# Every second first-layer product tile of a fused attention and FFN kernel moves to another PSUM bank, from unit 34 on

## The chip, the core and the metric

One core of one Trainium2 chip runs the whole program. The metric is the device time of one execution in microseconds. The engines are named as in the profile: PE multiplies matrices, PEld is its weight load, DVE is the vector engine, ACT the scalar engine, POOL the general-purpose engine and SP the engine that issues most transfers.

## What is computed

```python
scores = (1.0 / np.sqrt(D)) * np.matmul(q, k.transpose(0, 1, 3, 2))     # B, H, S, D = 4, 8, 576, 64
x = (np.log1p(abs(pos_i - pos_j)) / np.log1p(max(pos_i, 1)))[..., None]
bias = np.maximum(x @ w1 + b1, 0.0) @ w2                                # 576 x 576, 8 heads, 32 hidden
scores = scores + bias.transpose(2, 0, 1)[None]
attn = softmax(scores)
x = np.matmul(attn, v)                    # heads joined: 4 x 576 rows of 512
xn = (x - mu) / np.sqrt(var + 1e-06) * g_ln
out = x + np.maximum(xn @ w_ch1, 0.0) @ w_ch2                           # 512 -> 2048 -> 512
```

## The kernel before, in words

The 576 query rows of a batch are cut into four chunks of 128 and a tail of 64. A *unit* is one batch, one chunk and one head (for a tail, two heads); there are 144. For each unit `qk` makes the score products (L391, tile `sps`, two buffers of two banks), DVE adds the bias and takes the minimum (L434), ACT takes the exponential (L438) and a half-precision copy (L443), DVE makes the remainder of that copy (L462, L464), a transfer transposes both (L470) and `pv` multiplies by the values (L480, tile `xps`, one bank). `pv` of a unit stands three, from unit 38 four units behind. When the eight heads of a chunk are through, the 128 rows are scaled (L516, for tails L543) and normalised and become one of 18 *blocks*.

The FFN works on a block in four jobs. A job is a first-layer tile and a second-layer step. `ffn_w1` accumulates 48 products of 128 columns into one 128 x 512 PSUM tile `hps` (L709), ACT writes its ReLU in half precision to `hh` (L714), and DVE writes the remainder of that rounding (L717, the closure `lo`, called a step later). Only then is the bank of `hps` free. `ffn_w2` multiplies `hh` by the second-layer weights in 12 products of 512 columns into the tile `y` (L736, tag `y0`), and DVE adds `y` to the residual (L747). `ffn_micro` alternates the two: with two tiles open the older one's `ffn_w2` comes before the next `ffn_w1`. There are 72 `hps` tiles in all.

The bias is made in 36 groups of 16 rows. `bias_relu` fills four `r` tiles on DVE and ACT; in the next step `bias_mm` multiplies them (L181: eight product instructions, 32 output partitions each), and two ACT instructions move the result to `ev` (L187), which goes to memory (`nb`) and is read back per unit as `ldb`. The tiles `r`, `ev` and the softmax tile `t` share one pool of seven buffers. From the 13th group on a group of at most 512 columns is held in the PSUM tag `y1`; the last such group comes near unit 100.

PSUM is full: four banks for `sps`, one for `xps`, one with the tag `h`, one with `y0`, one with `y1`. Before the change the tag `h` holds every `hps` tile (and a few small ones), and `y1` holds sums over the weights at the start and then these bias products only.

The program is written unit by unit. A planner of the tile framework then lays out each engine's order when the kernel is built: an instruction whose buffer or input is not there by the planner's own clock is passed by later ones of the same engine. On the chip that order is fixed, and each engine takes its instructions in it.

Of the kernel before, what the change touches and what calls it, by code (L numbers as in the profile page):

```python
# [8 lines left out]
F32 = mybir.dt.float32  # L9
# [13 lines left out]
def kernel(  # L23
# [35 lines left out]
    ps_h = ctx.enter_context(tc.tile_pool(name="ps_h", bufs=1, space=bass.MemoryType.PSUM))  # L59
    ps_y = ctx.enter_context(tc.tile_pool(name="ps_y", bufs=1, space=bass.MemoryType.PSUM))  # L60
# [545 lines left out]
    ustep = [-1]  # L606
# [89 lines left out]
        V.tensor_scalar(out=gs_sb, in0=gs_sb, scalar1=gsc, scalar2=4.0, op0=ALU.mult, op1=ALU.mult)  # L696
        V.tensor_scalar(out=ginv, in0=ginv, scalar1=0.25, scalar2=None, op0=ALU.mult)

    yps = {}

    def ffn_w1(k, fs):
        n = 128 * len(blocks[k])
        h = ps_h.tile([128, 512], F32, tag="h", name="hps")
        for idx, f in enumerate(fs):
            w = wslot[f].bitcast(F16)
            i = 0
            for kk in range(4):
                for wo, xo in ((0, 0), (0, 4), (512, 0)):
                    T.matmul(out=h[:, idx * n:idx * n + n],  # L709
                             lhsT=w[:, wo + kk * 128:wo + kk * 128 + 128],  # L710
                             rhs=xT[k][:, xo + kk, 0:n], start=(i == 0), stop=(i == 11))
                    i += 1
        hh = hp.tile([128, 2, 512], F16, tag="h", name="hh")
        S.activation(hh[:, 0], h, AF.Relu)  # L714

        def lo():
            V.scalar_tensor_tensor(out=hh[:, 1], in0=h, scalar=0.0, in1=hh[:, 0],  # L717
                                   op0=ALU.max, op1=ALU.subtract)

        return [k, fs, hh, lo]  # L720
# [62 lines left out]
    def ffn_micro(u):  # L783
        if state["w1"] and len(pend) > 1:
            k, fs, hh, _ = pend.pop(0)
            ffn_w2(k, fs, hh)
            state["w1"] = False
            return True
        kf = next_fs(u)
        if kf:  # L790
            flush_lo()
            pend.append(ffn_w1(*kf))
            state["lo"] = pend[-1][3]
            state["w1"] = True
            return True
        if pend:
            flush_lo()
            k, fs, hh, _ = pend.pop(0)
            ffn_w2(k, fs, hh)
            state["w1"] = False  # L800
            return True
        return False
# [189 lines left out]
```

## Time and profile before

| what | value |
|---|---|
| three runs | 683.54, 686.28, 686.31 us (median 686.28) |
| profiled execution | 679.99 us, of which the span from first to last instruction is 678.2 us |
| mean granted TensorE clock | 0.985 of 2.4 GHz |
| PE busy | 647.7 us (96% of the span) |
| DVE, ACT, POOL busy | 457.8, 392.0, 97.4 us |

Busy times are sums over the whole span. A share of the span is an average over stretches with different limits, so the stretches are looked at one by one. Unit 34 begins at about 192 us, where its L434 starts.

### The profile page before, as it was taken

How to read it: one execution, taken by the hardware profiler on the slowest of the kernel's cores; microseconds unless marked ns; L12 is line 12 of the kernel's file. 1: busy time of each engine (PE TensorE's matmuls, PEld its weight loads, DVE VectorE, ACT ScalarE, POOL GpSimd, SP SyncE). 2: the span in 40 equal slices, each digit the busy share in tenths (PEclk: the TensorE clock that was granted, in tenths of full speed). 3: DMA queues.
4: the chain of work that ended last, by engine and by line, in shares of the span. 5: the costliest groups of instructions: out<-in, count | busy, mean ns of one | idle time of the engine just before them, and what ended most of it. 6: DMA issues, size and time to landing. Idle time of an engine off the chain costs nothing.

```text
span 678.2 us, 19142 instructions
## 1 busy us (share of the span) xinstructions
PE 647.7 (96%) x7929; PEld 448.4 (66%) x7929; DVE 457.8 (68%) x1061; ACT 392.0 (58%) x777; POOL 97.4 (14%) x163
## 2 busy tenths in 40 slices
PE   6889996998999889999899999999999999999997
PEld 4447774676466666666667766666776677677775
DVE  6588999778757567686766575757576676766322
ACT  5565847478957447787764577576554455444110
POOL 5312321011000011111101110111011120000000
PEclk9989997899999999999899999999999999999999
DMA  8999885444659996868869789789996976744100
GB/s 312 294 404 331 307 294 161 143 91 115 143 122 148 223 246 156 173 156 164 172 149 239 134 183 181 136 197 181 201 200 144 166 153 125 121 98 87 33 16 17
DMA packets 186955, 117.24 MB, mean 173 GB/s; under 512 B 163956, under 2 KB 164084, under 8 KB 186868
## 3 DMA queue, kind: packets, MB, share of 16 engines
q1 hardware_dynamic: 177124, 81.00, 55.8%
q0 software_dynamic: 9600, 34.84, 16.6%
q8 instruction: 62, 1.02, 0.6%
q10 hardware_dynamic: 144, 0.18, 0.1%
q14 instruction: 25, 0.20, 0.1%
HBM read 60.51 MB, written 15.63 MB: 112 GB/s over the span
## 4 chain that ended last, share of the span: by engine, by line
PE 50%; DVE 0%; ACT 0%; issue 0%
PE hps L709 19%; PE y L736 18%; PE sps L391 6%; PE xps L480 6%; PE bps L181 1%; DVE v L369 0%; DVE x L747 0%; DVE e L462 0%; ACT e L443 0%; DVE x L516 0%; ACT t L438 0%; DVE e L464 0%
## 5 line engine op out<-in xcount | busy, mean ns | idle before, releaser
L709 PE MATMUL hps<-xT,w 128*128 128x128 f16 x3240 | 196.4, 220 | 5.8 <-DVE hh L717 2.6
L709 PEld LDWEIGHTS <-w 128*128 128x128 f16 x3240 | 184.6, 98 | 11.5 <-issue 5.2
L736 PE MATMUL y<-w,hh 128*128 128x512 f16 x810 | 189.1, 381 | 1.9 <-ACT hh L714 1.8
L438 ACT ACTIVATE t<-t,m 128x576 f32<-128x576 f32 x144 | 111.0, 771 | 132.8 <-DVE m L434 132.2
L736 PEld LDWEIGHTS <-hh 128*128 128x128 f16 x864 | 79.7, 98 | 90.6 <-ACT hh L714 3.3
L462 DVE SCALAR_TENSOR_TENSOR e<-t,e 128x512 f16<-128x512 f32 x120 | 82.8, 690 | 81.8 <-ACT e L443 81.5
L434 DVE CUSTOM_DVE_ANT_0 t<-sps,ldb 128x576 f32<-128x576 f32 x144 | 105.9, 753 | 31.4 <-PE sps L391 21.2
L391 PE MATMUL sps<-kf,qf 64*128 64x288 f32 (+1 forms) x640 | 96.6, 436 | 3.5 <-DVE m L434 3.5
L443 ACT ACTIVATE e<-t 128x576 f16<-128x576 f32 x120 | 80.8, 679 | 9.8 <-DMA pt<-e 3.5
L714 ACT ACTIVATE hh<-hps 128x512 f16<-128x512 f32 x72 | 42.0, 583 | 53.4 <-PE hps L709 47.9
L717 DVE SCALAR_TENSOR_TENSOR hh<-hps,hh 128x512 f16<-128x512 f32 x72 | 49.4, 687 | 34.0 <-ACT hh L714 33.5
L391 PEld LDWEIGHTS sps<-kf,qf 64*128 64x128 f32 (+1 forms) x640 | 48.2, 176 | 35.6 <-issue 17.5
L480 PEld LDWEIGHTS <-pt 128*128 128x128 f16 (+1 forms) x1456 | 49.3, 100 | 30.5 <-issue 24.9
L747 DVE SCALAR_TENSOR_TENSOR x<-y,ycs,x 128x512 f32<-128x512 f32 x58 | 43.4, 748 | 32.2 <-PE y L736 32.0
L480 PE MATMUL xps<-v,pt 128*128 128x64 f16 (+1 forms) x1456 | 59.0, 195 | 1.9 <-DMA pt<-e 1.1
L291 POOL DMA_DIRECT2D kf<-in_k_s_dram x56 | 31.1, 556 | 161.4 <-PE sps L391 114.3
L304 POOL DMA_DIRECT2D qf<-in_q_main_dram x32 | 18.5, 577 | 162.4 <-PE xps L480 82.6
L187 ACT ACTIVATE ev<-bps,cb_sb,par_sb 128x144 f32<-128x144 f32 (+27 forms) x48 | 26.0, 593 | 26.2 <-PE bps L181 26.0
L160 ACT ACTIVATE r<-psi_sb,par_sb 128x448 f32<-128x448 f32 (+23 forms) x72 | 39.7, 614 | 0.0
L569 POOL TENSOR_SCALAR rs<-mv 128x1 f32<-128x1 f32 x18 | 9.9, 549 | 146.3 <-DVE mv L568 138.3
L438 ACT ACTIVATION_READ_ACCUMULATOR t<-t,m 128x1 f32 x144 | 27.0, 188 | 0.0
L181 PE MATMUL bps<-r,nw_sb 128*32 128x448 f32 (+24 forms) x200 | 26.9, 494 | 0.0
(121 smaller groups left out, 641.4 us busy)
## 6 DMA issues: line engine op xcount, KB each, us to landing
kf<-in_k_s_dram POOLq DMA_DIRECT2D x56, 288.0 KB, 4.8
w<-in_w_ch_dram SPq DMA_DIRECT2D x22, 512.0 KB, 8.7
ldb<-nb SPq DMA_DIRECT2D x32, 288.0 KB, 4.5
qf<-in_q_main_dram POOLq DMA_DIRECT2D x32, 256.0 KB, 4.6
nb<-ev SPq DMA_DIRECT2D x24, 296.0 KB, 3.4
vf<-in_v_p_dram POOLq DMA_DIRECT2D x16, 320.0 KB, 7.5
out_dram<-x SPq DMA_DIRECT2D x18, 256.0 KB, 2.1
wend<-in_w_ch_dram SPq DMA_DIRECT2D x8, 512.0 KB, 4.8
```

The costliest lines, as they stand in the source:

```text
L160: S.activation(r[:, 0:n], psi_sb[:, 0:n], AF.Relu, bias=pr_sb[:, g4:g4 + 1], scale=1.0)
L391: m = T.matmul(out=o, lhsT=l, rhs=kk, start=True, stop=True, tile_position=(64 * hf, 64 * e))
L434: ttri[u] = V.tensor_tensor_reduce(out=halves(t), in0=ps[:, :, 0:HS], in1=halves(bias), scale=-0.125, scalar=3e38, op0=ALU.add, op1=ALU.mi ...
L438: S.activation(t, t, AF.Exp, bias=m, scale=-1.0, accum_out=l8[b, c][:, h:h + 1])
L443: S.activation(e16[:, 0:SEQ], t, AF.Copy, scale=E_SCALE)
L462: V.scalar_tensor_tensor(out=e16[:, 640:1152], in0=t[:, 0:512], scalar=E_SCALE, in1=e16[:, 0:512], op0=ALU.mult, op1=ALU.subtract)
L480: T.matmul(out=o, lhsT=p[:, m], rhs=v[:, j, a, :], start=(i == 0), stop=(i == len(ops) - 1))
L709: T.matmul(out=h[:, idx * n:idx * n + n], lhsT=w[:, wo + kk * 128:wo + kk * 128 + 128], rhs=xT[k][:, xo + kk, 0:n], start=(i == 0), stop=( ...
L714: S.activation(hh[:, 0], h, AF.Relu)
L717: V.scalar_tensor_tensor(out=hh[:, 1], in0=h, scalar=0.0, in1=hh[:, 0], op0=ALU.max, op1=ALU.subtract)
L736: T.matmul(out=yps[k][t], lhsT=hh[:, a, o:o + 128], rhs=w[:, wo:wo + 512], start=(f == f0 and i == 0), stop=(f == f1 - 1 and i == 2))
L747: V.scalar_tensor_tensor(out=x, in0=y, scalar=ycs[:, g:g + 1], in1=x, op0=ALU.mult, op1=ALU.add)
```

## The change

The tiles of `ffn_w1` are counted. While the unit counter is at 34 or more, each one with an even number takes the PSUM bank of the tag `y1` in place of `h`. No instruction is added or taken away.

```diff
-    yps = {}
+    yps, hn = {}, [0]
 
     def ffn_w1(k, fs):
         n = 128 * len(blocks[k])
-        h = ps_h.tile([128, 512], F32, tag="h", name="hps")
+        hn[0] += 1
+        if ustep[0] >= 34 and hn[0] % 2 == 0:
+            h = ps_y.tile([128, 512], F32, tag="y1", name="hps")
+        else:
+            h = ps_h.tile([128, 512], F32, tag="h", name="hps")
         for idx, f in enumerate(fs):
```

## Rows read from the trace of the kernel before

**Rows 1.** Busy time by stretch: length, engines, clock, DMA share, GB/s.
```profile
192.00:336.00 144.00, 138.47 (x1861) 93.59 (x1859) 98.41 (x234) 99.40 (x202) 18.00 (x31) 0.99 0.84 173
336.00:480.00 144.00, 144.00 (x1839) 99.93 (x1837) 94.23 (x220) 91.34 (x180) 18.81 (x32) 0.99 0.84 174
480.00:678.20 198.20, 194.39 (x2458) 139.06 (x2455) 110.69 (x245) 76.10 (x149) 17.77 (x27) 1.00 0.57 113
...
330.00:340.00 10.00, 8.00 (x113) 6.30 (x110) 8.77 (x19) 7.21 (x13) 2.11 (x3) 0.83 0.83 148
```

**Rows 2.** PE's waits from 192 us on: us in total, times, longest.
```profile
PE hps L709 <- DVE hh L717: 2.6, 2, 1.3
PE y L736 <- ACT hh L714: 1.6, 1, 1.6
```

**Rows 3.** Chain that ended last, two units near 512 us: start, us, what.
```profile
511.87 1.17 PE sps L391 x8
513.04 0.52 PE xps L480 x14
513.56 2.68 PE hps L709 x48
516.24 0.41 PE xps L480 x14
516.64 2.59 PE y L736 x12
```

**Rows 4.** Timeline near 517 us, how the tile of rows 3 is emptied.
```profile
516.37 0.58 ACT L714 ACTIVATE hh<-hps 128x512 f16<-128x512 f32 x1
517.24 0.68 DVE L717 SCALAR_TENSOR_TENSOR hh<-hps,hh 128x512 f16<-128x512 f32 x1
```

**Rows 5.** Timeline 223 to 237 us, the first wait for the bank.
```profile
223.80 0.58 ACT L714 ACTIVATE hh<-hps 128x512 f16<-128x512 f32 x1
224.67 0.69 DVE L717 SCALAR_TENSOR_TENSOR hh<-hps,hh 128x512 f16<-128x512 f32 x1
225.41 2.84 PE L709 MATMUL hps<-xT,w 128*128 128x128 f16 x48 [1.28 <-DVE hh L717]
...
230.21 2.01 SPq L470 DMA_TRANSPOSE wend<-e  x1
...
236.10 0.63 PE L480 MATMUL xps<-v,wend 128*64 128x64 f16 x28 [0.53 <-DMA wend<-e]
```

**Rows 6.** Timeline 250 to 254 us, the second wait for the bank.
```profile
250.19 2.17 PE L709 MATMUL hps<-xT,w 128*128 128x128 f16 x36 [1.30 <-DVE hh L717]
250.72 0.75 DVE L434 CUSTOM_DVE_ANT_0 t<-sps,ldb 128x576 f32<-128x576 f32 x1
251.39 0.75 DVE L434 CUSTOM_DVE_ANT_0 t<-sps,ldb 128x576 f32<-128x576 f32 x1
252.46 0.86 DVE L543 TENSOR_TENSOR x<-xps,rl 64x256 f32<-64x256 f32 x2
253.47 0.63 PE L480 MATMUL xps<-v,pt 128*64 128x64 f16 x28 [0.43 <-DVE x L543]
```

**Rows 7.** All first-layer remainders from 192 us on: busy, mean ns, idle before.
```profile
L717 DVE SCALAR_TENSOR_TENSOR hh<-hps,hh 128x512 f16<-128x512 f32 x64 | 44.0, 687 | 32.8 <-ACT hh L714 32.3
```

**Rows 8.** PE's groups from 336 to 472 us, the bias products.
```profile
L181 PE MATMUL bps<-r,nw_sb 128*32 128x385 f32 (+7 forms) x64 | 7.6, 545 | 0.0
```

**Rows 9.** Timeline, bias products behind a first-layer tile, first and last of six.
```profile
203.60 0.80 PE L181 MATMUL bps<-r,nw_sb 128*32 128x352 f32 x8
205.56 0.69 DVE L717 SCALAR_TENSOR_TENSOR hh<-hps,hh 128x512 f16<-128x512 f32 x1
...
462.20 1.04 PE L181 MATMUL bps<-r,nw_sb 128*32 128x497 f32 x8
462.94 0.69 DVE L717 SCALAR_TENSOR_TENSOR hh<-hps,hh 128x512 f16<-128x512 f32 x1 [0.96 <-ACT hh L714]
463.18 0.58 PE L480 MATMUL xps<-v,pt 128*128 128x64 f16 x14
```

**Rows 10.** Timeline near 349 us, a bias group ahead of a tile.
```profile
349.58 1.09 ACT L187 ACTIVATE ev<-bps,cb_sb,par_sb 128x384 f32<-128x384 f32 x2 [2.67 <-PE bps L181]
350.75 1.45 PE L709 MATMUL hps<-xT,w 128*128 128x128 f16 x23
```

**Rows 11.** Bias additions on DVE from 192 us on, and what they waited for.
```profile
L434 DVE CUSTOM_DVE_ANT_0 t<-sps,ldb 128x576 f32<-128x576 f32 x110 | 80.4, 753 | 25.4 <-PE sps L391 21.2 <-DMA nb<-ev 3.9
```

## The prediction

> **What bounds the kernel now.** I read the busy times by stretch first, from 192 us, where the change can first act. PE is the engine to watch: it is busy for 138.47 of the 144 us up to 336 us, for all of the next 144, and for 194.39 of the last 198.2, and the missing 3.8 there are the last residual addition and the transfer of the result behind PE's last product [rows 1]. So from 192 us on PE is idle for 144 − 138.47 = 5.5 us that a change could give back, all of it before 336 us.
>
> A busy PE could still hide slack, so I looked at one period of the chain that ended last. Two units, one first-layer tile and one second-layer step take 1.17 + 0.52 + 2.68 + 0.41 + 2.59 = 7.37 us, with no hole between them; the first layer runs at 2.68 / 48 = 55.8 ns a product, the second at 2.59 / 12 = 216 ns [rows 3]. 128 columns at 2.4 GHz would be 53 ns and 512 would be 213 ns, so the products themselves leave about 5% and 1%.
>
> PE's waits come third. The wait that the second bank addresses is a first-layer product waiting for the DVE remainder of the tile before, which empties bank `h`: 2.6 us in two waits of 1.3. The one larger single wait, 1.6 us, is a second-layer product waiting for ACT's ReLU, and no bank frees that [rows 2].
>
> Why are there only two? In the period above the tile's last product ends at 516.24, its ReLU runs 516.37 to 516.95 and its remainder ends at 517.92 [rows 3, 4]. The next tile starts one period after this one, at 513.56 + 7.37 = 520.93. The bank has been free for 3.0 us by then: `pv`, the second layer and the next scores lie between.
>
> **The change, part by part.** *Removed:* no instruction; the wait for `h`. First wait: ACT's ReLU came late, at 223.80, the remainder at 224.67, and PE stood 1.28 us to 225.41 [rows 5]. With two banks the tile in question finds its bank long empty. But what is late next? PE's following wait is for the transpose into `wend`, issued at 230.21, which releases `pv` at 236.10 after 0.53 us of idle PE [rows 5]. If PE comes there 1.28 us earlier and the transpose does not, it stands 1.81 us and nothing is won. Second wait: 1.30 us, to 250.19. Between it and the next wait DVE works back to back (L434 at 250.72 and 251.39, then L543 at 252.46), and `pv` is released by that L543 at 253.47 after 0.43 us of idle PE [rows 6]. DVE would not be earlier, so PE would stand 1.73 us there. The saving is thus between 0 and 2.6 us. I take 0, the value that both next waits point to.
>
> *Added, bias products behind a tile:* bank `y1` now has two users. A bias group that follows an even-numbered tile must wait for that tile's remainder. I laid the old order over the new banks: six groups start on PE while an even tile is still in the bank. The first starts at 203.60, against a remainder that ends at 205.56 + 0.69 = 206.25: 2.65 us. The last starts at 462.20 against 462.94 + 0.69 = 463.63: 1.43 us [rows 9]. The four between give 1.43, 1.44, 1.43 and 1.01 in the same way, so 9.4 us if every group stood in its old place. Behind it in PE's queue would stand `pv` (0.58 us), then the second layer and the scores, which need none of this bank [rows 3, 9]. The first three of the six lie before 331 us, ahead of the 1.6 us wait on ACT, and can partly run out in it [rows 2]. The last three, after 336 us, have no idle time to run out in: 1.43 + 1.01 + 1.43 = 3.9 us.
>
> Lower bound: the planner knows the bank is taken and puts `pv` and the second layer ahead. 0.58 + 2.59 = 3.17 us of such work is more than the longest of these waits, 2.65, so the cost can be 0. Then the bias comes up to some 3 us later; it is read back many units later, and the four `r` buffers are held longer in a pool of seven. If that cover is gone, L434 waits for a buffer: it already did for 3.9 us in the whole stretch, and PE had no wait for it [rows 2, 11].
>
> *Added, tiles behind a bias group:* a tile in `y1` must wait for both L187 of the group before. Near 349 us these end at 349.58 + 1.09 = 350.67, and the tile began at 350.75, 0.08 us later [rows 10]. It fits in the old order, but barely.
>
> *Value taken:* between 0 and 9.4 us I go by how the planner's order has held for the same kind of hand-over. After 192 us the bank `h` passes from one tile to the next 63 times (64 tiles [rows 7]), and PE waited 2.6 us for it in all [rows 2]: 0.041 us a hand-over. In `y1` there are eight bias groups from 336 to 472 us (64 instructions, eight a group [rows 8]) and nine even tiles between them, so 17 hand-overs where PE has no other idle time: 17 × 0.041 = 0.7 us.
>
> *Moved:* no transfer and no DVE or ACT instruction is added, and none gets longer. After the last bias group, near unit 100, the second bank is used freely, in a stretch where PE waits for nothing.
>
> Sum on the profiled execution: 679.99 − 0 + 0.7 = 680.7 us. That execution lies 6.3 us below the median of the runs shown, so I add the change to the median: 686.28 + 0.7 = 687.0 us. A difference of 0.5%, 3.4 us, is about the least that can be told here: the runs shown lie 2.8 us apart, and the profiled one further off.
>
> **Rule and row.** The trace shows a bank hand-over with 3.0 us to spare in the steady period [rows 3, 4]. The Trainium skill, "TensorE: Matmul & The Clock Gate", section "HAM oscillation — how this bites in real kernels", reports that double-buffering PSUM gave a kernel that was already kept busy no further gain (126.6 against 125.5 us, 0.9%). The rows agree so far; by that rule alone the sum would stay where it is.
>
> The same skill, "Perfetto Trace Analysis", section "Matmuls" under "Optimizing Tensor Performance", says the opposite for a case like this: rotate independent product groups through different banks, so that emptying one overlaps the next. By that rule the forecast would be the first rival's. The trace bears it out at two places in 486 us.
>
> **The rivals.**
> 1. *Faster: the second bank loosens the planner's order.* First-layer tiles no longer wait for the bank on the planner's clock either, so they can fill every hole that PE has before 336 us. All 5.5 us go, and with them the drop of the clock that the holes near 331 us bring: between 330 and 340 us the granted clock is 0.83 [rows 1], so 10 × (1 − 0.83) = 1.7 us are lost. Gain 5.5 + 1.7 = 7.2 us: 679.1. For it: the order is laid anew from unit 34, and runs slower than the profiled one may have more such holes. Against it: at 331 us `ffn_w2` follows its own tile with no other tile open, so there is nothing to fill in, and after 336 us there is no hole at all. It counts as faster from 3.4 us, about half of it.
> 2. *Slower: bias products stand at the head of PE's queue.* The place is the six groups above; the price is 9.4 us if the planner's clock frees the bank earlier than the chip does, as it did for the tile of the wait at 224 us, whose remainder came late: 695.7. With the last three alone it is 3.9 us: 690.2. It decides from 3.4 us, a little over a third of 9.4. Against it: later products are free to go ahead.
> 3. *No effect at all:* the planner's order stays as it is and each hand-over fits: 686.3, which is the same verdict as the forecast.
>
> **How the numbers follow.** The forecast with rival 3 gets 0.53: PE is full after 336 us, and both waits that go are followed by waits that PE does not set. Faster gets 0.25: a new order may close more holes than the two. Slower gets 0.22: hand-overs that fit by 0.08 us can slip. The predicted time is 687.0. The range runs from rival 1's 679 to 692, a little over rival 2's smaller case, and leaves out its full 9.4 us; within the forecast's own case it is 683.5 to 690.
>
> **What would show it.** In the trace after, the waits of first-layer products for L717 near 224 and 250 us should be gone and the next waits of `pv` longer by about as much. Bias products should stand behind `pv` or second-layer products where they followed a tile. New waits of L181 for L717, or of L709 for L187, should sum to under 2 us after 336 us. PE should be as busy after 336 us, with the same end. The prediction is wrong if PE's idle time between 192 and 336 us falls well below 5.5 us with the span shorter by as much (rival 1), or if L181 stands on PE for more than 3 us in all (rival 2). A new order on DVE or ACT, with PE waiting for scores or transposes, would be a cause that I have not priced.

## The result, and the profile after

The changed kernel takes 692.17 us in the median of six runs (689.74 to 695.26), against 684.60 us for six runs of the kernel before (681.02 to 686.31): a ratio of 1.0133 with a 95% interval from 1.0089 to 1.0178. It is slower by 1.3%, about 9 us. The forecast was 687.0 us and no difference; the median lies just above its range. In the file after, the lines from `ffn_w1` on are four higher: products L713, ReLU L718, remainder L721, second layer L740, residual L751.

The profiled execution took 695.26 us with a span of 693.5 us, 15.3 us more than the profiled span before. Where do they arise? The additions of the bias on DVE mark the units. First the kernel before, from unit 34 on: count, shortest, median and longest in ns, then the first and the last start in us.

```profile
L434 DVE CUSTOM_DVE_ANT_0 t<-sps,ldb x110: 747/753/759, 192.2 to 616.9; 128x576 f32<-128x576 f32 x110
```

The same view of the kernel after:

```profile
L434 DVE CUSTOM_DVE_ANT_0 t<-sps,ldb x110: 743/752/759, 194.3 to 632.2; 128x576 f32<-128x576 f32 x110
```

Unit 34 starts 194.3 − 192.2 = 2.1 us later, before the change can act: that much belongs to these two executions, not to the change. The 110 additions take 437.9 us in place of 424.7, so 13.2 us arise behind it. Behind the last addition both need 61.3 us (678.2 − 616.9 and 693.5 − 632.2). By the starts of single units the stretch from unit 104 to unit 140, behind the last bias group, is also the same, 132.9 us before and 132.8 after. So the second bank used freely costs nothing and gains nothing there, where PE waited for nothing before either. The whole loss lies ahead of unit 104: 2.9 us in units 34 to 47, 6.5 in 48 to 72 and 4.5 in 80 to 103, while units 73 to 79, which have no bias group, took 0.7 us less. These are single executions. From unit 34 to unit 104 the kernel before took 283.3 us, and two experiments below in which PE has nearly the same order, e1 and e13, took 279.9 and 279.7; the kernel after took 296.5.

The busy time by stretch of the kernel after answers to [rows 1]; columns as there:

```profile
194.00:336.00 142.00, 133.78 (x1790) 90.38 (x1788) 90.51 (x217) 92.06 (x192) 16.45 (x30) 0.99 0.82 167
336.00:480.00 144.00, 138.64 (x1720) 94.09 (x1721) 90.43 (x210) 84.87 (x167) 17.71 (x31) 0.99 0.82 166
...
357.00:361.00 4.00, 3.44 (x14) 1.51 (x15) 2.22 (x7) 3.97 (x9) 0.00 (x0) 0.62 0.37 82
```

PE stood for 8.2 us up to 336 us and for 5.4 us in the next 144, where before it had stood for none: 13.6 against 5.5, so 8.1 of the 13.2 us are idle time. The other 5.1 us are time in which PE is busy for longer: 654.2 us in all, 6.5 more than before, 1.3 of it ahead of unit 34. The third line shows one source: for four microseconds behind a long wait the granted clock was 0.62 of 2.4 GHz, so for most of them it was at the lower level, 1.2 GHz. The kernel after has a second such stretch (0.66 from 258 to 263 us), but the kernel before had one too (0.83 from 330 to 340 us [rows 1], where the kernel after has 1.00), so the clock makes a difference of one stretch, about 1.7 us. The larger source is the bias products. This is their line in the kernel before (busy, mean ns of one, idle before):

```profile
L181 PE MATMUL bps<-r,nw_sb 128*32 128x448 f32 (+24 forms) x200 | 26.9, 494 | 0.0
```

and in the kernel after:

```profile
L181 PE MATMUL bps<-r,nw_sb 128*32 128x448 f32 (+24 forms) x200 | 29.9, 495 | 6.7 <-DVE hh L721 3.4 <-ACT r L160 3.2
```

One product takes as long as before, but together they keep PE busy for 3.0 us more, since at a few places the eight products of a group are pulled apart and overlap less. I did not account for what is left.

PE's waits from 194 to 480 us in the kernel after (us in total, times, longest) answer to [rows 2]:

```profile
PE bps L181 <- DVE hh L721: 3.4, 2, 2.0
PE bps L181 <- ACT r L160: 3.2, 1, 3.2
PE xps L480 <- DVE x L543: 2.3, 1, 2.3
PE xps L480 <- DMA wend<-e: 2.0, 1, 2.0
PE hps L713 <- DMA xT<-x: 1.0, 1, 1.0
PE y L740 <- DVE x L751: 0.7, 1, 0.7
```

The waits of a first-layer product for the remainder, 2.6 us, are gone. In their place bias products wait 6.6 us, half for a tile's remainder and half for their own input `r`, and `pv` waits 4.3 us for a transpose and for DVE.

The timeline of the kernel after shows three of these places:

```profile
323.86 0.83 PE L713 MATMUL hps<-xT,wend 128*128 128x128 f16 x12
...
329.19 0.57 ACT L718 ACTIVATE hh<-hps 128x512 f16<-128x512 f32 x1
...
330.80 0.80 PE L181 MATMUL bps<-r,nw_sb 128*32 128x353 f32 x8 [1.37 <-DVE hh L721]
...
356.89 0.62 ACT L160 ACTIVATE r<-psi_sb,par_sb 128x385 f32<-128x385 f32 x1 [4.91 <-DMA nb<-ev]
357.56 1.10 PE L181 MATMUL bps<-r,nw_sb 128*32 128x385 f32 x2 [3.19 <-ACT r L160]
...
465.12 1.01 PE L181 MATMUL bps<-r,nw_sb 128*32 128x481 f32 x8 [2.02 <-DVE hh L721]
```

The first is what the forecast priced for a bias group behind an even tile, 1.0 to 2.65 us at each of six groups [rows 9]. The bias does not stand right behind the tile: the planner had put a second-layer step, scores and part of `pv` between. But the tile's last product ended at 324.69, and its ReLU, behind other work in ACT's order, came only at 329.19, so the remainder ended 6.05 us after the product. The second is not a wait for the bank at all. ACT stood 4.91 us, because `r` needs one of the pool's seven buffers and the next one to come free held an `ev` that was still being written to memory. The third looks like the first, but the chain that ended last leads further back (start, us, what):

```profile
454.99 1.19 ACT r L160 x2
...
456.20 4.30 DMA nb<-ev
...
460.63 0.13 DVE t L434
...
464.46 0.61 DVE hh L721
...
465.12 1.01 PE bps L181 x8
```

L434 on DVE needed a buffer of the same pool, which the write held to 460.5 us; the exponential and the copy on ACT and the halves of that copy on DVE followed, the remainder that empties the bank came behind them, and behind the remainder stood the bias products on PE. Before the change this chain had no place on the path: ACT's `r` waited for no buffer, and the 3.9 us of L434 [rows 11] did not reach PE.

### The profile page after: what moved, and what is told of

Read it like the earlier page. It is cut to its first block, busy times and chain, and to the rows that moved or that the text cites. A ratio compares the mean times of both kernels' runs of the same rounds, so it can differ in the third digit from the quotient of the medians.

```text
span 693.5 us, 19132 instructions
## 1 busy us (share of the span) xinstructions
PE 654.2 (94%) x7929; PEld 449.6 (65%) x7929; DVE 456.2 (66%) x1061; ACT 390.7 (56%) x777; POOL 95.8 (14%) x163
## 5 line engine op out<-in xcount | busy, mean ns | idle before, releaser
L713 PE MATMUL hps<-xT,w 128*128 128x128 f16 x3240 | 197.9, 220 | 4.2 <-DVE w L686 2.5
L740 PE MATMUL y<-w,hh 128*128 128x512 f16 x810 | 192.1, 385 | 1.1 <-DVE x L751 0.7
L713 PEld LDWEIGHTS <-w 128*128 128x128 f16 x3240 | 184.5, 98 | 13.2 <-issue 4.8
L740 PEld LDWEIGHTS <-hh 128*128 128x128 f16 x864 | 80.4, 99 | 90.9 <-issue 6.5
L434 DVE CUSTOM_DVE_ANT_0 t<-sps,ldb 128x576 f32<-128x576 f32 x144 | 105.7, 751 | 27.5 <-PE sps L391 14.6
L721 DVE SCALAR_TENSOR_TENSOR hh<-hps,hh 128x512 f16<-128x512 f32 x72 | 49.4, 686 | 44.8 <-ACT hh L718 44.5
L718 ACT ACTIVATE hh<-hps 128x512 f16<-128x512 f32 x72 | 42.1, 584 | 52.2 <-PE hps L713 46.7
L751 DVE SCALAR_TENSOR_TENSOR x<-y,ycs,x 128x512 f32<-128x512 f32 x58 | 43.3, 747 | 33.7 <-PE y L740 33.7
L187 ACT ACTIVATE ev<-bps,cb_sb,par_sb 128x144 f32<-128x144 f32 (+27 forms) x48 | 26.0, 592 | 34.7 <-PE bps L181 34.7
L181 PE MATMUL bps<-r,nw_sb 128*32 128x448 f32 (+24 forms) x200 | 29.9, 495 | 6.7 <-DVE hh L721 3.4
```

Of the source, the lines that this page charges most:

```text
L434: ttri[u] = V.tensor_tensor_reduce(out=halves(t), in0=ps[:, :, 0:HS], in1=halves(bias), scale=-0.125, scalar=3e38, op0=ALU.add, op1=ALU.mi ...
L713: T.matmul(out=h[:, idx * n:idx * n + n], lhsT=w[:, wo + kk * 128:wo + kk * 128 + 128], rhs=xT[k][:, xo + kk, 0:n], start=(i == 0), stop=( ...
L740: T.matmul(out=yps[k][t], lhsT=hh[:, a, o:o + 128], rhs=w[:, wo:wo + 512], start=(f == f0 and i == 0), stop=(f == f1 - 1 and i == 2))
L751: V.scalar_tensor_tensor(out=x, in0=y, scalar=ycs[:, g:g + 1], in1=x, op0=ALU.mult, op1=ALU.add)
```

## The experiments

Each ratio is to the kernel before, in runs on the same chip, with its 95% interval. Where two experiments are compared I divide their ratios; such a quotient is uncertain by 0.4 to 0.5 points. All kernels compute the whole reference.

### Only where no bias group meets a tile (e1), and only where they meet (e2, e5)

Only the condition in `ffn_w1` differs; the three added lines are e1, e2 and e5 in this order.

```diff
-        if ustep[0] >= 34 and hn[0] % 2 == 0:
+        if (40 <= ustep[0] < 48 or 73 <= ustep[0] < 80 or ustep[0] >= 104) and hn[0] % 2 == 0:
...
+        if (48 <= ustep[0] < 73 or 80 <= ustep[0] < 104) and hn[0] % 2 == 0:
...
+        if 34 <= ustep[0] < 48 and hn[0] % 2 == 0:
```

> Second bank only in units 40 to 47, 73 to 79 and from 104 on, where no bias group holds it; the order planned for every engine is that of before up to the last tiles. Theory A (conflict: tiles and bias groups in one bank make bias products late, and that is what costs): within 0.4% of before. The waits of first-layer products for L721 near 224 and 250 us are gone, and the waits of values products after them are longer by about 1.3 us each, so that PE's idle time from 192 to 336 us stays at 4.5 to 6 us. Theory B (loose order: a second bank lets first-layer products go ahead of scores and values, sharing or not): 2 to 4 us slower. Theory C (the wait removed is worth its 2.6 us): 2 to 3 us faster.

> Second bank only in units 48 to 72 and 80 to 103, where bias groups hold it too. Theory A: most of the loss of the full change, 5 to 11 us slower than before, with waits of L181 on PE for L721 or L160 of 4 us or more. Theory B: about the share of the units, 48 of 110, so 3 to 5 us slower.

> Second bank only in units 34 to 47, where the last two or three bias groups of the first batch of groups share it. Run e2 (the later shared units) was 0.7% slower, the full change 1.3%. Theory A (sharing): the rest is here, 3 to 5 us slower than before, the bias groups near units 36 and 39 several us later on PE than before. Theory D (the loss grows with the number of shared groups alone, 3 here against 15 in e2): about 1 us slower.

Measured: e1 0.9999 [0.9970, 1.0028], e2 1.0072 [1.0041, 1.0103], e5 1.0062 [1.0034, 1.0090]. The two shared parts make 1.34% together, the whole 1.33%, each uncertain by 0.3 to 0.5 points; the unshared stretches make nothing that can be measured. So the loss comes from the sharing. e2 alone would not show this, since its 4.9 us fit both theories, and its waits of L181, 2.1 us, are fewer than I had expected. The loss is also not only a wait at the bank: in the profiled execution of e5 PE never waits with L181. Its two largest waits there, from 192 to 500 us, are for transposes:

```profile
PE xps L480 <- DMA wend<-e: 2.3, 1, 2.3
PE hps L713 <- DMA xT<-x: 1.2, 1, 1.2
```

The kernel after has the same two, of 2.0 and 1.0 us. They stand in units 34 to 47, where the planner laid a new order around the shared bank; what in that order makes them was not tested.

e1 also tests what the removed wait was worth. Its timeline on PE:

```profile
233.74 2.84 PE L713 MATMUL hps<-xT,w 128*128 128x128 f16 x48 [1.41 <-DVE hh L721]
...
260.00 0.63 PE L480 MATMUL xps<-v,pt 128*64 128x64 f16 x28 [0.54 <-DVE x L543]
```

The first wait stays, since its tile is made before unit 40. The second, of 1.30 us [rows 6], is gone, and the next `pv` waits 0.54 us where it waited 0.43: here the 1.3 us were not given back at the place that I had named. PE's waits from 192 to 500 us fall from 5.5 us before to 3.5 in e1, while I had expected them to stay at 4.5 to 6. Such a gain is 0.2 to 0.3% of the run, no more than the interval can tell.

### One more buffer in the pool (e3, e4, e8)

`r`, `ev` and `t` get eight buffers in place of seven; the pool `xt` gives up one of four for it. e3 is the kernel before with this, e4 the kernel after, e8 is e1.

```diff
-    ep = ctx.enter_context(tc.tile_pool(name="e", bufs=7))
+    ep = ctx.enter_context(tc.tile_pool(name="e", bufs=8))
-    xtp = ctx.enter_context(tc.tile_pool(name="xt", bufs=4))
+    xtp = ctx.enter_context(tc.tile_pool(name="xt", bufs=3))
```

> The kernel before with eight buffers in place of seven in the pool of the softmax tile t, the bias tiles r and the tile ev, paid for by three in place of four buffers of the transposed rows xT. Control of the next run. Theory A: the same as before, minus 1 to plus 1 us, as PE has no wait for the pool in the old order.

> The changed kernel with the same eight buffers. Theory A1 (late bias groups hold the pool, so that softmax tiles and the next r tiles wait for the write of ev): at most 4 us slower than the control, the wait of ACT's L160 for the write of ev (5.5 us) gone. Theory A2 (bias products stand on PE for the bank itself): 7 to 10 us slower than the control, as without the buffer.

> The second bank only where no bias group lives, as in e1, with eight buffers in the pool as in e3. Theory A: as e3, 0.2 to 0.6% faster than before; the bank adds less than 0.2% to the buffer. Theory C (the wait removed is worth its time): 0.5 to 0.8% faster than before.

Measured: e3 0.9971 [0.9947, 0.9994], e4 1.0015 [0.9990, 1.0041], e8 0.9955 [0.9926, 0.9984]. With the eighth buffer the change costs 1.0015 / 0.9971 = 1.0044 in place of 1.0133. e8 against e3, 0.9984, cannot tell whether the removed wait is worth its time. ACT's wait for a buffer ahead of `r` is gone in e4. PE's waits that are left there, from 190 us on:

```profile
PE sps L391 <- DVE m L434: 1.4, 2, 1.0
PE hps L713 <- ACT ev L187: 1.1, 2, 0.8
PE bps L181 <- DVE hh L721: 0.6, 1, 0.6
```

By this pair the eighth buffer takes away a good part of the loss, and waits at the bank itself, in both directions, stay. But two things change at once: with the eighth buffer the planner also lays out another order for PE, from the kernel before to e3 and from the kernel after to e4, as their traces show. And the pair e17 and e18 below, with the same eight buffers, does not repeat the gain.

### Bias groups in the score buffers (e6, e7, e11, e12)

All bias products go to the tag of `sps`. In e6 every `hps` stays in `h`; in e7 every second one has `y1` to itself. e12 is e6 with eight buffers; e11 is a second look at the kernel of e6, not a new one.

```diff
-        if gi in gorder[12:] and n <= 512:
+        if False:
...
-            flat = ps if n <= 512 else ps.rearrange("p a b -> p (a b)")
+            flat = ps.rearrange("p a b -> p (a b)")
```

> Control of the next run: all tiles of first-layer products in the bank h, and every bias group held in the two-bank buffers of the scores (tag s), so that y1 stands empty after the start. Slower than before by 2 to 12 us, since a bias group now takes one of two score buffers.

> The same with every second first-layer tile in y1 from unit 34 on, which nothing else uses. Theory A (sharing is what costs): the same as the control or up to 3 us faster. Theory B (a loose order costs): slower than the control by 4 us or more.

> One more look at the control of e7, for a second profile: 34 to 140 stretch as there.

> All tiles in the one bank h, bias groups in the score buffers as in e6, eight buffers as in e3: if the two small gains add, 0.4 to 0.6% faster than before; if both only remove the same waits, 0.2 to 0.3%.

Measured: e6 0.9978 [0.9949, 1.0008], e7 1.0017 [0.9988, 1.0046], e12 0.9985 [0.9961, 1.0009]; the one run of e11 took 677.14 us, and from unit 34 to unit 140 its profile has 413.9 us, as that of e6 has. I had expected e6 to be slower by 2 to 12 us, and it is not. e7 against e6, +0.39%, is within the uncertainty: no gain is seen from two banks that nobody shares. The pair says no more. The eighth buffer gains 0.3% on the kernel before; on e6 no gain is seen, but the uncertainty does not rule out the same 0.3%.

### Few shared tiles, and how late the bias comes (e9, e10)

Only one unit in three gives tiles to `y1`. In the planned order half of the bias groups come 1.5 us later in e9 and the other half 3.4 us later in e10. The theory was that the delay of the bias sets the loss. The first added line is e9, the second e10.

```diff
-        if ustep[0] >= 34 and hn[0] % 2 == 0:
+        if 48 <= ustep[0] < 72 and ustep[0] % 3 == 0 or 80 <= ustep[0] < 103 and ustep[0] % 3 == 2:
...
+        if 48 <= ustep[0] < 72 and ustep[0] % 3 == 1 or 80 <= ustep[0] < 103 and ustep[0] % 3 == 0:
```

> One tile in every three units, between units 48 and 71 and 80 and 102, in the second bank, a unit or two before the next bias group. In the planned order of PE half of the bias groups then stand behind the next scores and nine values products, 1.5 us later (1.17 + 0.35); the other half stand where they did, and the scores are not moved later. Theory A as dose (the later the bias products, the larger the loss): 0.0 to 0.3% slower than before. Theory E (any sharing of the bank costs the same per tile): as the next run.

> As many tiles, but each in the step right before the bias group. In the planned order the other half of the groups stand behind values products and a whole second-layer step, 3.4 us later (0.41 + 2.59 + 0.35), and the scores behind them are moved into the middle of the next first-layer tile. Theory A as dose: 0.6 to 1.3% slower than before, with waits for the write of ev above 5 us. Theory E: as the run before.

Measured: e9 1.0172 [1.0126, 1.0217], e10 1.0081 [1.0050, 1.0111]. The shorter delay costs more, so the theory fell. By the starts of single units e9 took 8.1 us more than the kernel before in units 70 to 75 of the profiled execution, in one event. Its timeline from 338 us on:

```profile
336.95 6.85 SPq L470 DMA_TRANSPOSE pt<-e  x2
...
337.82 0.53 ACT L187 ACTIVATE ev<-bps,cb_sb,par_sb 128x224 f32<-128x224 f32 x1
...
343.85 0.59 SPq L211 DMA_DIRECT2D nb<-ev  x1
...
349.41 0.62 ACT L160 ACTIVATE r<-psi_sb,par_sb 128x385 f32<-128x385 f32 x1 [7.86 <-DMA nb<-ev]
...
353.20 0.57 ACT L718 ACTIVATE hh<-hps 128x512 f16<-128x512 f32 x1
...
354.24 0.68 DVE L721 SCALAR_TENSOR_TENSOR hh<-hps,hh 128x512 f16<-128x512 f32 x1
...
354.98 1.51 PE L181 MATMUL bps<-r,nw_sb 128*32 128x385 f32 x8 [5.76 <-DVE hh L721]
```

Read from above: `ev` is ready at 338.35, but its write stands in SP's queue behind two transposes until 343.85. `r` waits for the buffer on ACT until 349.41. The ReLU of a tile stands behind `r` in ACT's order, so it comes at 353.20. The remainder follows, then the bank is free, and PE, which had the bias products at the head of its queue, has stood 5.76 us. Behind it the clock falls too: from 354 to 358 us the granted clock is

```profile
354.00:358.00 4.00, 3.02 (x25) 1.79 (x26) 2.93 (x8) 1.37 (x3) 0.00 (x0) 0.53 0.79 148
```

0.53, which is nearly all at 1.2 GHz. So a bias group that is hardly late can cost much where other work stands behind it and it meets a late write. This is one event in one execution, which at 688.82 us is also 3.5 us faster than the median of e9; e15 and e16 below show what becomes of it.

### The write out of the queue of the transposes (e13, e14, e15)

All writes of `ev` are issued by POOL. e13 is the kernel before with this, e14 the kernel after, e15 is e9.

```diff
-        (G if gi in gorder[0:12] else SY).dma_start(out=dst, in_=ev[:, 0:ntot])
+        G.dma_start(out=dst, in_=ev[:, 0:ntot])
```

> The kernel before with the writes of ev issued by POOL in place of SP for the later groups too; PE's planned order is that of before. Control of the next two. Theory F (the loss comes where the write of ev stands behind transposes in SP's queue and a chain of ACT, DVE and the shared bank hangs on it): within 0.4% of before, which has no such chain to PE.

> The changed kernel with the same writes on POOL; PE's planned order is that of the changed kernel. Theory F: no more than 0.6% slower than the control, ACT's wait of L160 for the write of ev under 2 us. Theory G (the planned order of PE itself costs, whatever the writes do): 1.0 to 1.5% slower than the control.

> e9 with the writes on POOL; PE's planned order is that of e9. Theory F: the 5.8 us wait of PE near unit 71 is gone or under 1.5 us, and the run within 0.6% of the control. Theory G: 1.4 to 2.0% slower than the control, as e9 was against before.

Measured: e13 0.9973 [0.9944, 1.0002], e14 1.0069 [1.0040, 1.0097], e15 1.0078 [1.0034, 1.0122]. The cost of the change falls from 1.33% to 0.96% (1.0069 / 0.9973), that of e9 from 1.72% to 1.05%, and the wait of 5.76 us falls to 1.75. The first difference is within what two pairs can tell, the second is at its edge. That the queue takes part is seen in the profile for the one event: units 70 to 75 take 23.4 us in e15, where e9 took 30.3 and the control e13 22.5. It is not all: in e14 ACT's `r` waits for no buffer any more, and the cost of 0.96% lies between the two theories. The 1.05% of e15 cannot be put down to the bank from its profile: its largest wait, 4.0 us for a transpose at 229.9 us, stands ahead of its first shared tile.

### Eight buffers with the few shared tiles (e16), and both remedies together (e17, e18)

e16 is e9 with eight buffers. e17 is the kernel before with eight buffers and the writes on POOL, e18 the kernel after with both.

> e9 with eight buffers, writes on SP. Theory F: r finds a buffer without waiting for the write, so the wait near unit 71 is gone and the run is 0.0 to 0.4% above e3, the kernel before with eight buffers (0.3% faster than before). Theory G: 1.0% or more above e3.

> The kernel before with eight buffers (e3) and the writes of ev on POOL (e13) together; the planned orders of PE, DVE and ACT are those of e3. Control of the next run and the fastest candidate without the second bank: 0.3 to 0.6% faster than before.

> The changed kernel with both; PE's planned order is that of e4. Theory F (pool and write carry the loss): 0.0 to 0.3% slower than the control, PE's waits of L181 under 1 us. Theory G (sharing costs also without them, by PE's order and by the bank itself): 0.4 to 0.8% slower than the control, as e4 was against e3.

Measured: e16 1.0079 [1.0049, 1.0110], e17 0.9936 [0.9907, 0.9966], e18 1.0031 [0.9999, 1.0063]. e17 beats both kernels: 677.11 us in the median, against 681.93 for the kernel before on the same chip. e18 against e17 is still +0.96%; I had expected at most 0.3%, so the theory that pool and queue are the whole loss fell. e16 had said the same: against e3 it is +1.08%, where this theory gave at most 0.4%. Its timeline shows why the eighth buffer did not help there:

```profile
349.96 0.76 DVE L434 CUSTOM_DVE_ANT_0 t<-sps,ldb 128x576 f32<-128x576 f32 x1 [6.17 <-DMA nb<-ev]
...
350.78 1.24 PE L391 MATMUL sps<-kf,qf 64*128 64x288 f32 x8 [2.83 <-DVE m L434]
```

`r` now finds a buffer, but the next one that is needed is that of `t`. L434 waits 6.17 us for the late write of `ev`, as `r` did in e9, and PE waits for L434. So one more buffer moved the wait to the next user of the pool.

Part of what is left in e18 can be read from the profiles of e17 and e18, whose spans are 673.6 and 678.6 us. PE's waits of e18 from 192 to 500 us:

```profile
PE hps L713 <- ACT ev L187: 2.5, 2, 1.8
PE bps L181 <- DVE hh L721: 2.4, 2, 1.7
PE sps L391 <- DVE m L434: 0.3, 1, 0.3
PE xps L480 <- DMA pt<-e: 0.3, 1, 0.3
```

The same view of e17:

```profile
PE hps L709 <- DVE hh L717: 0.5, 1, 0.5
PE xps L480 <- DVE x L516: 0.4, 1, 0.4
PE xps L480 <- DVE x L543: 0.4, 1, 0.4
PE xps L480 <- DMA pt<-e: 0.4, 1, 0.4
```

4.9 us of e18 are hand-overs of the shared bank, tile to bias and bias to tile, and e17 has none of either. But e17 has 1.7 us of other waits where e18 has 0.6, so the waits explain 3.8 us net; between unit 34 and unit 104 the two lie 6.0 us apart (one execution of each). One of the hand-overs in e18, on all engines:

```profile
297.85 2.84 PE L713 MATMUL hps<-xT,w 128*128 128x128 f16 x48
...
304.56 2.56 PE L713 MATMUL hps<-xT,w 128*128 128x128 f16 x43
...
306.69 0.72 ACT L596 ACTIVATE x<-u,rs 128x512 f16<-128x512 f32 x1 [4.00 <-DMA pt<-e]
307.32 0.58 ACT L718 ACTIVATE hh<-hps 128x512 f16<-128x512 f32 x1
...
308.12 0.68 DVE L721 SCALAR_TENSOR_TENSOR hh<-hps,hh 128x512 f16<-128x512 f32 x1
...
308.86 0.78 PE L181 MATMUL bps<-r,nw_sb 128*32 128x337 f32 x8 [1.73 <-DVE hh L721]
```

The same bias group in e17, on PE:

```profile
304.32 2.84 PE L709 MATMUL hps<-xT,w 128*128 128x128 f16 x48
307.10 0.77 PE L181 MATMUL bps<-r,nw_sb 128*32 128x337 f32 x8
```

In both the bias stands right behind the tile that begins near 304 us. In e17, with a bank of its own, it starts at once. In e18 that tile is an odd one, in `h`, and the bias waits for the even one before it, which holds `y1`. Its last product, the 43rd of those at 297.85, ended at 300.41. But its ReLU stands behind L596 in ACT's order, and L596 waited 4.00 us for a transpose. So the ReLU comes at 307.32 and the remainder ends at 308.80, 8.4 us after the product; 1.73 us of that reach PE. Another of the four, 1.75 us, still has the pool in it: L187 there waited 1.75 us for a write of `ev`. From 192 to 500 us such a write lands in 4.1 us in the median from POOL in e18 and in 4.0 us from SP in the kernel after, so the move does not make the write itself faster. That the writes on POOL are no full cure may explain part of the missed expectation.

## Why the prediction was wrong

**What held.** PE bounds the kernel. After unit 104 nothing changes. That the removed waits save nothing was not shown: e1 gives 0.9999 ± 0.003, which leaves room for the 1.3 us that it removed. At the two waits that followed the removed ones, for `wend` and for L543, I had worked out 1.81 and 1.73 us if the removed time came back there; the kernel after has 1.99 and 2.30. That agrees, but it is no proof, since PE's order differs there; in e1, with the order nearly unchanged, the wait at the second place grew by 0.1 us and not by 1.3. The loosened order of rival 1 did not come: PE stood more before 336 us, not less.

**The step that failed** is the value taken for the bias products behind a tile. I had bounds of 0 and 9.4 us and chose 0.7, by the price that hand-overs of `h` had before: 0.041 us each. That is a mean over hand-overs which mostly had time to spare, 3.0 us in the steady period, and it says nothing of a place where the remainder comes late. In place of 0.7 us the runs show a loss of about 9 us, and within the uncertainty all of it where the two share the bank (e2 and e5). In the profile the bias products wait 6.6 us and run for 3.0 us longer, against the 3 us of waits that the forecast named as a sign of being wrong. Sign and place are those of rival 2, and its mechanism, bias products at the head of PE's queue, came at two of its six groups: 1.37 us at 330 us where 1.44 had been worked out, and 2.02 at 465 us for 1.01. At the other four L181 does not wait. So at most 3.4 us are of the kind that rival 2 priced, and that the loss comes out near its 9.4 us is luck.

**The lower bound's cover failed as well.** I had `pv` and the second layer go ahead, and the bias come later at no cost, since L434 "already did" wait for a buffer without reaching PE [rows 11]. The planner did put all six groups behind a second-layer step. For the first of them PE runs (timeline of the kernel after):

```profile
206.47 1.96 PE L713 MATMUL hps<-xT,w 128*128 128x128 f16 x32
...
210.20 1.50 PE L713 MATMUL hps<-xT,w 128*128 128x128 f16 x24
211.64 0.80 PE L181 MATMUL bps<-r,nw_sb 128*32 128x352 f32 x8
```

The group of 203.60 [rows 9] comes at 211.64, 5.9 us later without the 2.1 us of before, and 45 of the 48 products of the next tile, in `h`, are ahead of it. But the 3.17 us of such work were set against remainders at their old times, and these came later too: at the two groups that wait, the remainder ends 6.05 and 6.51 us after the tile's last product, where the same two tiles had 4.37 and 3.93 before. The path there leads through things that I had not followed: the pool of seven, the write of `ev` in SP's queue, and the fixed orders of ACT and DVE, in which a ReLU stands behind `r` or other work and a remainder behind the halves of the softmax copy. Both longer waits of L181 in the kernel after, 3.19 and 2.02 us, have the pool in their chain.

**"Nothing moved" was too narrow.** No instruction was added, but the planner laid the engines' orders anew around the new bank. I named a new order as a cause that I had not priced; the one profile of e5, with waits for transposes and none of L181, points to it. The hand-over that I thought the closest, a tile behind a bias group, is no wait in the kernel after, and 2.5 us in e18.

**Size.** Of the 1.33%, the eighth buffer takes away 0.9 points and the write on POOL 0.4, but both together also only 0.4, each uncertain by 0.5 to 0.6 points. With the pool eased, 0.44 points (e4) or 0.96 points (e18) of the cost stay. How the loss divides between waits at the bank, the pool and the new order stays open.

**Rules and rows.** Where the second bank is shared with nobody, the ratio is 0.9999 (e1). The Trainium skill, "TensorE: Matmul & The Clock Gate", section "HAM oscillation — how this bites in real kernels", reports no further gain from double-buffering PSUM in a kernel that had been rebuilt so that PE stays warm; this agrees. The Trainium skill's rule to rotate product groups through banks ("Perfetto Trace Analysis", "Matmuls" under "Optimizing Tensor Performance") would let one expect a gain, the first rival's. No gain was seen: PE waited for the bank for 2.6 us [rows 2], and with a bank that had a user already the ratio was 1.0133.

## What to carry to other kernels

Before a buffer gets a second kind of user, count how long PE waits for it now, here 2.6 of 486 us, and price the new waits by the whole hand-over (product end, ReLU, remainder) at each place where the two meet, not by the mean of hand-overs that have time to spare. A hand-over lasted 1.4 us at the least here, and 6 to 10 us where the bias waited longest for it, since the engines that empty the bank had other work in front. Such a price holds for this kind of wait alone: four of the six groups did not wait, and the rest of the loss came by other ways. Then follow each late step through every shared pool and every in-order queue until it reaches the bound engine; a wait that reaches nobody today is no proof that it will not after the order has moved. The better step here was another: one more buffer and the writes away from the transposes gave 0.9936 [0.9907, 0.9966] without the second bank. Whether that comes from the loosened chain or from the order that the planner lays out with eight buffers was not tested.

## What the runs showed of the hardware that I had not expected

A write stood 5.5 us in SP's queue behind two transposes that occupied it for 6.85 us, although its data was ready (e9). A PE wait of 3.19 us was followed by a stretch of four microseconds at 0.62 of the full clock, one of 5.76 us by a stretch at 0.53, so these waits cost more than their own length. The two waits of 1.73 and 1.75 us in e18 had no such stretch behind them: the clock is 1.00 from 306 to 316 us and from 216 to 226.
